# Threshold attention and MLP mixer on one core: values moved up in the unit loop, token chunk padded to 128 rows

## The chip, the cores and the metric

The kernel runs on one core of a Trainium2 chip. The metric is the device time of one execution in microseconds (us). TensorE is called PE below (PEld is its weight load), VectorE DVE, ScalarE ACT, GpSimd POOL; SP is the engine that issues most DMAs. A name with a q (SPq, ACTq) is the sequencer of that engine.

## What is computed

All data is float32; B = 8 batches, H = 8 heads, S = 576 tokens, D = 64 per head, so 512 features per token.

```python
scores = q @ k.T / 8                              # per batch and head, 576 x 576
thresh = max(scores, -1) - tau                    # tau = 0.02
scores = where(scores >= thresh, scores, -1e9)
attn = exp(scores - max(scores)); attn /= sum(attn) + 1e-9
x = (attn @ v)   ->  (B, S, 512), heads side by side
u = x + (relu(x.T @ w_tok1) @ w_tok2).T           # token MLP, 576 -> 256 -> 576
out = u + relu(u @ w_ch1) @ w_ch2                 # channel MLP, 512 -> 1536 -> 512
```

The weights are random, and each is read once from memory and kept on the chip. Where a weight arrives as 64-bit floats it is converted on the chip by ACT, DVE and POOL (`f64_to_f32`, L145).

## The kernel before, in words

**Units.** The attention is cut into 144 units (L85): for each batch b ("row" in this document), for each half of its four head pairs, nine units t = 0 to 8. A unit is one block of 128 query tokens of one head pair; t = 4 is shared: it holds the last 64 tokens of two pairs. A row therefore has 18 units. One iteration of the main loop (L513) emits, in this order, the following pieces of several units. Each engine runs what is emitted for it in order, so the order of emission is the order on each engine:

1. `scores(u)` (L272): matmuls of q by k for both heads, 64 rows high (the head size), into two PSUM tiles `sc`, and on DVE the row maximum (L291), on POOL the bias from it (L292). The pool of `sc` holds two tiles, so the next unit's scores wait until both tiles of this unit have been read (L301).
2. `norm(u - 1)` (L307): reciprocal of the row sums on DVE, the multiplication on POOL (L314).
3. For w = u - 2, from row 1 on, `turn_blocks(w)` (L341): a DVE transpose in blocks (T, L348); when a group of units is complete (units t = 1, 3, 4, 6, 8), 16 small DMAs on SP's queue (L358) that complete the transpose into a tile `eT`. Row 0 does this on PE instead (`turn`, L325). A finished group is put on the list `due`, with the iteration from which its values may be emitted: u + 2 from row 1 on, u + 1 in row 0 (L540).
4. `fill(0.4)` (L487): filler steps, see below.
5. `weight(...)`: steps of the weight conversion (L216), until all weights are there.
6. `weigh(u)` (L295): on ACT the threshold (Prelu, L301, the reader of `sc`) and the exponential (L304).
7. `fill(0.3)`.
8. The groups that are due: `values(b, p, c)` (L370): 20 PE instructions of v by `eT`, 128 rows by 64 columns, for two heads beside each other (L388, L393; a shared group has two such calls with shorter operands, tile `pv_s`), and on ACT the copy of the result (L398). After the last group of a row `push(b)` (L497) is called.
9. `fill(0.3)`, `weight(...)`, and loads of later q, k and v.

**Filler.** The mixer of a finished row is a list of steps with costs in us as the planner assumes them: `turn_x` (L405, five transposes), `tok1` (L415, two), `tok2` (L425, eight), then `channel_mlp` in chunks of 256 tokens (L440: twelve `ch1`, and four parts of `ch2` for each 128 tokens). Two chunks follow an even row, three (the last one half as long) an odd row. `push` mixes the new token steps with what is left, sets a quota of total cost / 17 for each iteration, less 45 us in all that are kept back except after row 0, and `fill(share)` pays out share times quota. After the loop everything left is emitted (L569).

**The token MLP's first matmul.** `turn_x` makes a tile `x` with 576 tokens on partitions, as four chunks of 128 and a last one of 64 (`MT`, L59). `tok1` runs one matmul for each chunk, the last one with 64 rows:

```python
for t in range(NT):
    M = MT[t]
    nc.tensor.matmul(ps, lhsT=w1[0:M, t, P * m : P * m + P], rhs=s["x"][0:M, t, :], start=(t == 0), stop=(t == NT - 1))
```

One float32 matmul is two PE instructions in the trace.

Of the kernel before, what the change touches and what calls it, by code (L numbers as in the profile page):

```python
# [9 lines left out]
F32 = mybir.dt.float32  # L10
# [7 lines left out]
P = 128  # L18
# [3 lines left out]
def kernel(  # L22
# [26 lines left out]
    nc = tc.nc  # L49
    B, H, S, D = q.shape  # L50
    DM = H * D
# [73 lines left out]
    w2 = const.tile([P, NTK, S], F32, name="w2")  # L125
    wc1 = const.tile([P, NJ, NCC, P], F32, name="wc1")
    wc2 = const.tile([P, NJ, DM], F32, name="wc2")

# [132 lines left out]
    def prep(n):  # L263
        lq, lk = loaded.pop(n)
        made = []
        for src, name in ((lq, "qT"), (lk, "kT")):
            sb = work.tile([P, S], F32, tag=name, name=f"{name}_{n}")
            nc.vector.transpose(out=sb, in_=src.rearrange("p n d -> p (n d)"))
            made.append(sb)
        heads[n] = made  # L270

    def scores(u):  # L272
        b, p0, t = units[u]
        sc = [
            (ps_3rd if b == 0 and (2 * u + h) % 3 == 2 else ps_sc).tile([P, 2, MAIN], F32, tag="sc", name=f"sc{h}_{u}") for h in range(2)
        ]
        if t == SHARED:
            parts = [(b * NP + p0 + i, slice(MAIN, S), slice(64 * i, 64 * i + 64)) for i in range(2)]
        else:
            i, c = divmod(t - (t > SHARED), NI)  # L280
            parts = [(b * NP + p0 + i, slice(P * c, P * c + P), slice(0, P))]
        order = [(f, part, h) for f in range(2) for part in parts for h in range(2)]
        for f, (n, cols, rows), h in order if b else sorted(order, key=lambda o: o[2]):
            r = slice(D * h, D * h + D)
            qT, kT = heads[n]
            nc.tensor.matmul(sc[h][rows, f, 0:HS], lhsT=qT[r, cols], rhs=kT[r, HS * f : HS * f + HS], start=True, stop=True)  # L286
        mx = small.tile([P, 2], F32, tag="mx", name=f"mx_{u}")
        bias = small.tile([P, 2], F32, tag="bias", name=f"bias_{u}")
        for h in range(2):
            c = slice(h, h + 1)  # L290
            nc.vector.tensor_reduce(out=mx[:, c], in_=sc[h][:, :, 0:HS], axis=AX.XY, op=ALU.max)  # L291
            nc.gpsimd.tensor_scalar(out=bias[:, c], in0=mx[:, c], scalar1=toff, scalar2=-SCALE, op0=ALU.add, op1=ALU.mult)  # L292
        st[u] = sc, bias
# [76 lines left out]
    def values(b, p, c):  # L370

        lv, vl = vals[b * NP + p]
        if b not in xTs:
            xTs[b] = xTs[b + 1] = work.tile([P, NP, 2 * S], F32, tag="xT", name=f"xT_{b}")
        key = (b, p - p % 2, c) if c == "s" else (b, p, c)
        n, N, tok = (1, LAST, MAIN) if c == "s" else (2, 2 * P, 2 * P * c)
        first = LAST * (p % 2) if c == "s" else 0
        eT = eTs[key] if c == "s" else eTs.pop(key)
        if in_blocks(b):
            eT = eT[:, 0 : NK * n * P].rearrange("p (i c x) -> p c i x", i=4, c=NK)  # L380
            eT = eT[:, :, first // 32 : first // 32 + N // (32 * n), :]
        else:
            eT = eT[:, 0 : NK * n * P].rearrange("p (c x) -> p c x", c=NK)[:, :, first : first + N]
        ps = ps_tr.tile([P, MAIN], F32, tag="tr", name=f"pv_{b}_{p}_{c}")[:, 0:N]
        to = ps.rearrange("p (i x) -> p i x", x=32 * n) if in_blocks(b) else ps
        for h in range(2):
            r = slice(D * h, D * h + D)
            nc.tensor.matmul(to[r], lhsT=vl[:, r], rhs=eT[:, NI], start=True, stop=False, skip_group_check=True)  # L388
        for c in range(NI):
            for h in range(2):  # L390
                r = slice(D * h, D * h + D)
                j = (NI + 1) * h + c
                nc.tensor.matmul(to[r], lhsT=lv[:, j, :], rhs=eT[:, j], start=False, stop=(c == NI - 1), skip_group_check=True)  # L393
        x = xTs[b][:, p, S * (b % 2) + tok : S * (b % 2) + tok + N]
        if in_blocks(b) and n == 2:
            x = x.rearrange("p (n i x) -> p i n x", n=n, x=32)
            ps = ps.rearrange("p (i n x) -> p i n x", n=n, x=32)
        nc.scalar.copy(out=x, in_=ps)  # L398


    def token_mlp(b):
        xT = xTs.pop(b)
        o = S * (b % 2)
        s = {}

        def turn_x(t):
            M = MT[t]
            if t == 0:
                s["x"] = work.tile([P, NT, DM], F32, tag="x", bufs=1, name=f"x_{b}")
            ps = ps_tr.tile([P, MAIN], F32, tag="tr", name=f"tx_{b}_{t}").rearrange("p (c x) -> p c x", c=NP)  # L410
            for p in range(NP):
                nc.tensor.transpose(out=ps[0:M, p, :], in_=xT[:, p, o + t * P : o + t * P + M], identity=ident)  # L412
            nc.scalar.copy(out=s["x"][0:M, t, :], in_=ps[0:M].rearrange("q p d -> q (p d)"))

        def tok1(m):  # L415
            need(2)
            if m == 0:
                s["a"] = work.tile([P, NTK, DM], F32, tag="a", bufs=1, name=f"a_{b}")
            ps = ps_mm.tile([P, DM], F32, tag="mm", name=f"t1_{b}_{m}")
            for t in range(NT):  # L420
                M = MT[t]
                nc.tensor.matmul(ps, lhsT=w1[0:M, t, P * m : P * m + P], rhs=s["x"][0:M, t, :], start=(t == 0), stop=(t == NT - 1))  # L422
            nc.scalar.activation(out=s["a"][:, m, :], in_=ps, func=AF.Relu)

        def tok2(c, f):  # L425
            need(6)
            ps = ps_mm.tile([P, HS], F32, tag="mm", name=f"t2_{b}_{c}_{f}")
            for m in range(NTK):
                nc.tensor.matmul(  # L429
                    ps, lhsT=s["a"][:, m, P * c : P * c + P], rhs=w2[:, m, HS * f : HS * f + HS], start=(m == 0), stop=(m == NTK - 1)  # L430
                )
            u = xT[:, c, o + HS * f : o + HS * f + HS]
            nc.vector.tensor_add(out=u, in0=u, in1=ps)  # L433

        steps = [(0.44, lambda t=t: turn_x(t)) for t in range(NT)]
        steps += [(4.3, lambda m=m: tok1(m)) for m in range(NTK)]
        steps += [(0.97, lambda c=c, f=f: tok2(c, f)) for c in range(NCC) for f in range(2)]
        return steps
# [58 lines left out]
    def push(b):  # L497
# [8 lines left out]
            todo.extend(channel_mlp(b - b % 2, uT, i))  # L506
        quota = (sum(c for c, _ in todo) - (KEEP if b else 0.0)) / (UB - 1)

    prep(0)
    due = deque()  # L510
    b_now = 0
    LAG = 2
    for u in range(len(units) + LAG + 4):  # L513
        on = u < len(units)
        if u == UB:
            late.close()
            ps_mm = ctx.enter_context(tc.tile_pool(name="ps_mm", bufs=2, space=bass.MemoryType.PSUM))
        if on:
            b_now, p0, t = units[u]
            n = b_now * NP + p0  # L520
        w = u - LAG
        back = 0 <= w < len(units)
        if on:
            scores(u)
        if 0 < u <= len(units):
            norm(u - 1)
        if back:
            key, place, many = group_of(w)
            if in_blocks(key[0]):
                turn_blocks(w)  # L530
            else:
                for i in range(3):
                    turn(w, i)
            if place == many - 1:
                b, p, c = key
                if c == 0 and p % 2 == 0:
                    split_middle(b * NP + p)
                if c == "s":
                    split_middle(b * NP + p + 1)
                when = u + (2 if in_blocks(b) else 1)  # L540
                due += [(when, b, p + i, c) for i in range(2 if c == "s" else 1)]
        if b_now:
            fill(0.4)
        weight(4 if b_now else 1)
        if on:
            weigh(u)
        if b_now:
            fill(0.3)
        while due and due[0][0] <= u:
            _, b, p, c = due.popleft()  # L550
            values(b, p, c)
            if p == NP - 1 and c == 1:
                push(b)
        if b_now:
            fill(0.3)
        weight(3 if b_now else 1)
        if on:
            m = n + 2 + t // 4
            if t < 8 and m < len(pairs):
                load_qk(m, (nc.scalar if b_now else nc.sync,) * 2, t % 4)  # L560
                if t % 4 == 3:
                    load_v(m)
            if t == 2:
                prep(n + 1)
            if t == 7 and n + 2 < len(pairs):
                prep(n + 2)
# [31 lines left out]
```

## Time and profile before

| what | value |
|---|---|
| median of 3 runs | 1418.58 us (1417.44 to 1421.64) |
| the profiled execution | 1424.03 us |
| its span, first to last instruction | 1421.9 us |
| mean granted PE clock | 0.984 of full speed |
| PE busy | 1346.7 us, 95% of the span |
| PEld / DVE / ACT / POOL busy | 832.4 / 584.1 / 589.8 / 345.4 us |
| largest groups on PE | L451 `ch1` 406.2 us, L467 `ch2` 389.5, L286 scores 196.7, L393 values 124.0 |
| DMA | 128.34 MB in 257376 packets, mean 90 GB/s |

The page gives the busy time of each engine as a share of the span; the span in 40 slices with tenths of busy time; the chain of work that ended last; and the groups of instructions by source line with their mean length, the idle time of their engine just before them and what ended it. A matmul's recorded length includes the time that it takes to pass through the array, during which the next one already runs, so on PE the time from one start to the next is the price of an instruction, not its length.

### The profile page before, as it was taken

The numbers are of one execution on the slowest core, as the hardware profiler recorded it, in microseconds if no ns is written. First come the engines' busy times: TensorE is split into PE (matmuls) and PEld (weight loads), VectorE is DVE, ScalarE is ACT, GpSimd is POOL, SyncE is SP. The second block draws the span as 40 slices with busy tenths as digits, with TensorE's granted clock in tenths as the row PEclk, the third lists the DMA queues.
The fourth block names the chain that finished last, engine by engine and source line by source line (L and its number), as shares of the span: only waits on it lengthen the run. The fifth ranks groups of instructions, "written<-read, shape, count | busy, mean of one in ns | idle before, by whom it ended". The sixth has DMA issues, their size and how long they took to land.

```text
span 1421.9 us, 19495 instructions
## 1 busy us (share of the span) xinstructions
PE 1346.7 (95%) x6866; PEld 832.4 (59%) x6866; DVE 584.1 (41%) x1009; ACT 589.8 (41%) x1328; POOL 345.4 (24%) x681
## 2 busy tenths in 40 slices
PE   6777689988999999999999999999999999999998
PEld 4443455645656566565656566566657466566675
DVE  5888654344344443434433444334333443201000
ACT  5776353443545444353434444353334344220110
POOL 4565332222222222222212222222121222100000
PEclk9998899989999999999999999999999999999999
DMA  6344544443444434443343534443433433300000
GB/s 130 90 117 131 152 125 103 92 116 84 102 120 111 108 84 106 104 98 80 92 101 77 121 80 111 104 98 69 103 87 83 111 91 78 82 15 15 8 8 23
DMA packets 257376, 128.34 MB, mean 90 GB/s; under 512 B 208064, under 2 KB 221376, under 8 KB 257280
## 3 DMA queue, kind: packets, MB, share of 16 engines
q1 hardware_dynamic: 131632, 111.46, 29.9%
q10 hardware_dynamic: 125648, 15.64, 6.9%
q8 instruction: 55, 0.90, 0.3%
q14 instruction: 41, 0.34, 0.1%
HBM read 43.25 MB, written 9.44 MB: 37 GB/s over the span
## 4 chain that ended last, share of the span: by engine, by line
PE 81%; DVE 8%; SPq 5%; DMA 3%; ACT 3%; issue 1%; POOL 0%; DVEq 0%; ACTq 0%
PE c L467 26%; PE c L451 24%; PE sc L286 10%; PE pv L393 7%; SPq L358 5%; PE t L422 3%; PE t L429 3%; DVE mx L291 3%; PE pv L388 2%; DVE T L348 2%; PE tx L412 2%; PE c L463 1%; DMA eT<-T 1%; DMA scratch<-in_moe_w_ch_dram 1%; ACT e L301 1%
## 5 line engine op out<-in xcount | busy, mean ns | idle before, releaser
L451 PE MATMUL c<-xT,wc 128*128 128x256 f32 (+1 forms) x1920 | 406.2, 363 | 1.9 <-DVE xT L433 0.8
L291 DVE TENSOR_REDUCE mx<-sc 128x1 f32<-128x576 f32 x288 | 204.6, 751 | 489.5 <-PE sc L286 489.4
L467 PE MATMUL c<-wc,g 128*128 128x512 f32 x864 | 389.5, 597 | 0.0
L451 PEld LDWEIGHTS c<-xT,wc 128*128 128x128 f32 x1920 | 331.7, 190 | 75.9 <-issue 29.9
L292 POOL TENSOR_SCALAR bias<-mx,toff 128x1 f32<-128x1 f32 x288 | 76.7, 267 | 807.8 <-DVE mx L291 754.1
L301 ACT ACTIVATE e<-sc,bias 128x576 f32<-128x576 f32 x288 | 199.2, 741 | 169.7 <-POOL bias L292 148.8
L467 PEld LDWEIGHTS c<-wc,g 128*128 128x128 f32 x864 | 157.6, 190 | 177.3 <-issue 175.9
L452 ACT ACTIVATE g<-c 128x256 f32<-128x256 f32 (+1 forms) x240 | 87.3, 364 | 386.0 <-PE c L451 366.5
L304 ACT ACTIVATE e<-e,ntau 128x576 f32<-128x576 f32 x288 | 220.8, 774 | 0.0
L314 POOL TENSOR_SCALAR e<-e,rr 128x576 f32<-128x576 f32 x288 | 213.4, 753 | 17.3 <-DVE rr L311 4.1
L286 PE MATMUL sc<-kT,qT 64*128 64x288 f32 (+1 forms) x1280 | 196.7, 441 | 20.0 <-ACT e L301 10.9
L348 DVE STREAM_TRANSPOSE T<-e 128x1152 f32<-128x1152 f32 x126 | 172.5, 1369 | 16.5 <-DMA eT<-T 10.8
L286 PEld LDWEIGHTS sc<-kT,qT 64*128 64x128 f32 (+1 forms) x1280 | 107.1, 181 | 102.1 <-issue 50.1
L393 PE MATMUL pv<-eT,lv 128*64 128x256 f32 x1024 | 124.0, 385 | 0.0
L472 DVE COPY o<-c 128x512 f32<-128x512 f32 x36 | 24.6, 684 | 192.7 <-PE c L467 192.7
L393 PEld LDWEIGHTS pv<-eT,lv 128*64 128x64 f32 x1024 | 75.7, 140 | 38.0 <-issue 2.6
L429 PE MATMUL t<-w,a 128*128 128x288 f32 x256 | 78.8, 437 | 17.8 <-DVE xT L433 15.8
L422 PE MATMUL t<-x,w 128*128 128x512 f32 (+1 forms) x160 | 76.0, 613 | 0.0
L429 PEld LDWEIGHTS t<-w,a 128*128 128x128 f32 x256 | 46.7, 197 | 42.6 <-DVE xT L433 20.8
L398 ACT COPY xT<-pv 128x256 f32<-128x256 f32 x64 | 23.9, 373 | 107.4 <-PE pv L393 107.3
L433 DVE TENSOR_TENSOR xT<-xT,t 128x288 f32<-128x288 f32 x64 | 27.9, 442 | 96.5 <-PE t L429 96.4
L304 ACT ACTIVATION_READ_ACCUMULATOR e<-e,ntau 128x1 f32 x288 | 57.4, 199 | 0.0
(43 smaller groups left out, 600.4 us busy)
## 6 DMA issues: line engine op xcount, KB each, us to landing
eT<-T SPq DMA_DIRECT2D x896, 72.0 KB, 2.0
scratch<-in_moe_w_ch_dram SPq DMA_DIRECT2D x24, 512.0 KB, 3.8
lv<-in_v_dram SPq DMA_DIRECT2D x32, 288.0 KB, 3.3
out_dram<-o SPq DMA_DIRECT2D x36, 256.0 KB, 2.2
eT<-T SPq DMA_DIRECT2D x224, 36.0 KB, 1.9
lk<-in_k_dram ACTq DMA_DIRECT2D x108, 72.0 KB, 2.7
lq<-in_q_dram ACTq DMA_DIRECT2D x104, 72.0 KB, 2.1
lq<-in_q_dram SPq DMA_DIRECT2D x24, 72.0 KB, 3.3
```

The lines of the kernel that those rows point to most:

```text
L286: nc.tensor.matmul(sc[h][rows, f, 0:HS], lhsT=qT[r, cols], rhs=kT[r, HS * f : HS * f + HS], start=True, stop=True)
L291: nc.vector.tensor_reduce(out=mx[:, c], in_=sc[h][:, :, 0:HS], axis=AX.XY, op=ALU.max)
L301: nc.scalar.activation(out=eh, in_=sc[h][:, :, 0:HS], func=AF.Prelu, bias=bias[:, h : h + 1], scale=SCALE, alpha=STEEP)
L304: nc.scalar.activation(out=eh, in_=eh, func=AF.Exp, bias=ntau, accum_out=rs[:, h : h + 1])
L314: nc.gpsimd.tensor_scalar(out=eh, in0=eh, scalar1=rr[:, h : h + 1], scalar2=1.0, op0=ALU.mult, op1=ALU.mult)
L348: nc.vector.transpose(out=T.rearrange("p (a c n x) -> p c a n x", a=4, c=NK, n=n)[:, :, :, place, :], in_=e.rearrange("p (c a x) -> p c a ...
L393: nc.tensor.matmul(to[r], lhsT=lv[:, j, :], rhs=eT[:, j], start=False, stop=(c == NI - 1), skip_group_check=True)
L422: nc.tensor.matmul(ps, lhsT=w1[0:M, t, P * m : P * m + P], rhs=s["x"][0:M, t, :], start=(t == 0), stop=(t == NT - 1))
L429: nc.tensor.matmul(ps, lhsT=s["a"][:, m, P * c : P * c + P], rhs=w2[:, m, HS * f : HS * f + HS], start=(m == 0), stop=(m == NTK - 1))
L451: nc.tensor.matmul(ps, lhsT=wc1[:, j, c, :], rhs=uT[:, c, GR * i : GR * i + n], start=(c == 0), stop=(c == NCC - 1))
L452: nc.scalar.activation(out=s["g"][:, j, 0:n], in_=ps, func=AF.Relu)
L467: nc.tensor.matmul(flat, lhsT=s["g"][:, j, P * t : P * t + P], rhs=wc2[:, j, :], start=False, stop=(j == NJ - 1), skip_group_check=True)
```

## The change

Two edits are made. From row 1 on, the due values are emitted directly behind `scores(u)`, ahead of `norm`, `turn_blocks`, all filler and `weigh(u)`; `push` moves with them. In row 0 they stay where they were. The due times are not changed. And the last chunk of tokens is multiplied at full height, 128 rows: `x` becomes one fixed tile `x_sb` for all rows, and the upper 64 partitions of its last chunk, and those of `w1`, are set to zero once by POOL at the start.

```diff
+    x_sb = const.tile([P, NT, DM], F32, name="x_sb")
+    nc.gpsimd.memset(x_sb[LAST:P, NI, :], 0.0)
+    nc.gpsimd.memset(w1[LAST:P, NI, :], 0.0)
...
         def turn_x(t):
             M = MT[t]
-            if t == 0:
-                s["x"] = work.tile([P, NT, DM], F32, tag="x", bufs=1, name=f"x_{b}")
...
-            nc.scalar.copy(out=s["x"][0:M, t, :], in_=ps[0:M].rearrange("q p d -> q (p d)"))
+            nc.scalar.copy(out=x_sb[0:M, t, :], in_=ps[0:M].rearrange("q p d -> q (p d)"))
...
             for t in range(NT):
-                M = MT[t]
-                nc.tensor.matmul(ps, lhsT=w1[0:M, t, P * m : P * m + P], rhs=s["x"][0:M, t, :], start=(t == 0), stop=(t == NT - 1))
+                nc.tensor.matmul(ps, lhsT=w1[:, t, P * m : P * m + P], rhs=x_sb[:, t, :], start=(t == 0), stop=(t == NT - 1))
...
+    def mix(u):
+        while due and due[0][0] <= u:
+            _, b, p, c = due.popleft()
+            values(b, p, c)
+            if p == NP - 1 and c == 1:
+                push(b)
+
...
         if on:
             scores(u)
+        if b_now:
+            mix(u)
         if 0 < u <= len(units):
             norm(u - 1)
...
-        while due and due[0][0] <= u:
-            _, b, p, c = due.popleft()
-            values(b, p, c)
-            if p == NP - 1 and c == 1:
-                push(b)
+        if not b_now:
+            mix(u)
         if b_now:
             fill(0.3)
```

## The prediction, as put on record before the run

> **What bounds the kernel now.** I read the page first: busy times, slices, chain.
>
> ```profile
> PE 1346.7 (95%) x6866; PEld 832.4 (59%) x6866; DVE 584.1 (41%) x1009; ACT 589.8 (41%) x1328; POOL 345.4 (24%) x681
> PE   6777689988999999999999999999999999999998
> PEclk9998899989999999999999999999999999999999
> PE 81%; DVE 8%; SPq 5%; DMA 3%; ACT 3%; issue 1%; POOL 0%; DVEq 0%; ACTq 0%
> ```
>
> PE is full from about 200 us on; before that it waits for others. Next, the busy time by stage (columns: length, then busy time of PE, PEld, DVE, ACT, POOL with counts, PE clock, DMA share, GB/s):
>
> ```profile
> 100.00:205.00 105.00, 77.71 (x373) 49.06 (x372) 76.29 (x118) 57.63 (x119) 46.49 (x61) 0.85 0.50 138
> 300.00:310.00 10.00, 3.84 (x18) 2.29 (x20) 6.46 (x12) 5.85 (x12) 4.40 (x10) 0.69 0.62 158
> 480.00:810.00 330.00, 328.26 (x1694) 200.77 (x1693) 134.14 (x227) 137.31 (x314) 76.69 (x164) 1.00 0.40 95
> ```
>
> Up to 205 us (row 0 and the weight conversion) PE idles. At 300 to 310 us there is one hole, the end of row 1. Elsewhere a microsecond added to PE or taken from it is a microsecond of the span. So two things count: what PE's stream costs, and whether PE, which runs in order, meets a wait.
>
> The PE timeline of one iteration shows the stream:
>
> ```profile
> 600.15 1.24 PE L286 MATMUL sc<-kT,qT 64*128 64x288 f32 x8
> 601.32 3.72 PE L451 MATMUL c<-xT,wc 128*128 128x256 f32 x16
> 604.97 0.65 PE L388 MATMUL pv<-eT,vl 128*64 128x256 f32 x4
> 605.45 1.90 PE L393 MATMUL pv<-eT,lv 128*64 128x256 f32 x16
> 607.28 1.99 PE L451 MATMUL c<-xT,wc 128*128 128x256 f32 x8
> 609.20 1.20 PE L286 MATMUL sc<-kT,qT 64*64 64x288 f32 x16
> ```
>
> The numbers behind the line are the shape of the array in use: 64*128 for scores, 128*128 for filler, 128*64 for values. The starts of single instructions give the price of a change of shape. Inside a run of L451, starts lie 216 ns apart; from its last one to another shape 309 ns (+93); and the first one of a run is followed after 320 ns (+104). A change into full shape or into scores costs 93 + 104 = 197 ns, one into values 93 + 51 = 144 ns (261 for 210). From scores straight to values it is 333 ns for 242, the same 91.
>
> The other side is the DMA chain that values wait for, in the SP timeline and in the answer on L358:
>
> ```profile
> 605.21 11.10 SPq L358 DMA_DIRECT2D eT<-T  x16
> L358 SPq DMA_DIRECT2D eT<-T x1120: 507/589/1937, 136.8 to 1242.6; - x187
> DMA to landing us min/median/max: 1.8/2.0/5.5
> ```
>
> Sixteen issues take about 10 us; the last lands 2 us later. Over all 70 groups, first issue to last landing is 12.05 us on average (11.3 to 13.1). The first issue stands 4.31 us after the start of the scores of its iteration, nearly always. So values of iteration u can't start before s(u-2) + 16.4 us, with s the start of scores.
>
> **What the Trainium skill says.** "TensorEngine Tiling (Array Packing)", Key Properties: changing the tiling mode drains TensorE. The trace agrees: 93 ns at each change. "TensorE: Matmul & The Clock Gate", "What overlaps and what doesn't": weight loads overlap running matmuls only in other row groups; that page also has loads pulled ahead into a background buffer. The trace shows the overlap lost just behind a change of shape (+104). The same page, "Why this matters for your kernels": PE gaps above some 3 us bring the clock to half. Here the hole of 301 to 308 us did it (clock 0.69 in the table), gaps of 1.7 us at 338 and 346 us didn't.
>
> **The change, part by part.**
>
> *Shape changes.* Before, an iteration with values runs scores, filler, values, filler; after, scores, values, filler. One re-entry into filler goes: 197 ns. I followed the planner's costs and credit on paper through both orders: of the 70 iterations with values from unit 18 on, 47 have filler behind the values and save it; in 23 the order changes without fewer changes of shape. 47 x 0.197 = 9.3 us.
>
> *Full height.* The two forms of L422:
>
> ```profile
> L422 PE MATMUL t<-x,w 128*128 128x512 f32 x128 | 59.2, 606 | 0.0
> L422 PE MATMUL t<-x,w 64*128 64x512 f32 x32 | 18.0, 641 | 0.0
> ```
>
> By starts, full height costs 429 ns; the step into the 64-row pair 522, between its two instructions 533, out of it 519. Per `tok1` that is 93 + 104 in excess, and 90 + 51 or 104 more where no scores follow (scores have 64 rows too, no change). Afterwards a tok1 in front of scores pays 197 there. Summed over 16 calls: 4.5 before, 2.6 after, 1.9 us saved. In several places the last 64-row matmul overlapped with scores of the other half (a 14 ns start distance); that is lost, at most 0.43 x 4, say 1 us. Both together: 9.3 + 1.9 - 1 = **-10 us**. The two memsets: 128x128 takes 202 ns on POOL (L121); these are 64x512 and 64x256, at most 0.4 us each, while POOL waits for the first scores at 9 us: nothing, and 0.8 us without that cover.
>
> *Landing.* Values come at s(u) + 1.2 instead of behind 70% of the filler. The landing doesn't move, so iterations u-2 and u-1 must last 15.2 us together. Group by group in the trace of before, I compared landing and end of scores. The cover after the change is 2 to 5 us in rows 4 and 6, 0 to 3 in rows 3, 5 and 7, and missing in row 2, whose iterations are short (6.5 to 8 us without values). There the landing is late by 1.3, 2.2, 2.4, 4.2, 2.2 and 0.7 us (iterations 46, 48, 52, 53, 55, 57). A wait at one is a head start for a group already under way: 1.3 + 0.9 + 2.4 + 1.9 + 0.3 + 0.4 = 7.1 us. Walking the new filler slots with the prices above gives 8.4 in row 2, 5.9 in rows 3 to 7 (single waits of 0.3 to 1.8), and 4.6 at iterations 145 and 147, where no scores stand between: 18.9. About 1 us of this exists before (0.7 at 436 us). **+18 us**; with 11.5 us to landing +12, with 12.6 us +27. Moved instructions on SP: none, since turn_blocks and its DMAs stay behind scores. The wait stands in PE's queue, with the filler queued behind it, and on ACT behind the copy of the values.
>
> *ACT.* The copy L398 (373 ns) and its wait now come ahead of `weigh(u)`: Prelu starts about 1.5 us later, 2.3 where filler on ACT comes between. Exp still ends before the next norm needs it. The next scores need both Prelus done; before, 2.2 us of values hid them where all filler fell into the first slot. That cover is gone, 2 us each. But push comes 0.7 of an iteration earlier, so the long tok1 steps fall elsewhere; the walk finds one new wait (iteration 61, 1.8) and two of 0.4 gone: **+1 us**. Bounds: 0 to +8.
>
> *Row 0 and 1.* Push of row 0 is 0.7 of an iteration earlier, and PE has room there. By iteration 27 two more ch2 steps (5.2 us) are done, if the weights set the pace. Against it, filler runs out an iteration earlier at the end of row 1:
>
> ```profile
> 308.06 1.12 PE L388 MATMUL pv<-eT,vl 128*64 128x256 f32 x4 [4.93 <-DMA eT<-T]
> ```
>
> This wait of 4.9 us, with 2.0 ahead of it, grows to some 10. Net **-3 us** (between -4 and +2, if ACT's order holds up the weights).
>
> *Clock.* One or two more gaps of 3 us at half clock: **+1 us** (0 to +5).
>
> Sum: -10 + 18 + 1 - 3 + 1 = **+7 us**: the profiled 1424.0 becomes 1431. The median of the runs is 5.4 us below the profiled one; there, 1418.6 + 7 = **1425.6 us**.
>
> **Rivals.** *Shape changes win* (the other side): the place is rows 2, 3, 5 and 7; the price -10 - 3 against landing waits. The waits decide from about 13 us on; if they are 7, because landing takes 11.5 us and part of them replaces stalls that row 2 has anyway (1.7 us twice at 338 and 346 us, for the adds of tok2), it is -6: 1413 us. For it: 46 of the 68 groups that scores follow would have been in time with over 1 us to spare; the issues take 9.4 us when undisturbed. Against it: row 2 is short whatever happens. *Landing with half clock*: groups at 12.6 us (SP's issues slow to 10.5 us when q and k load), waits of 27, half clock twice: +9 more and some, 1436. For it: six groups of row 2 in the trace took 12.4 to 13.0. *They cancel*: waits of 12, 1419.
>
> **Chances.** Forecast 0.45, shape changes win 0.20, landing heavy 0.25, cancel 0.10. A measurement of this kernel can tell about 0.3%, 4.3 us, from no change. Slower by more: 0.33 of the forecast and the heavy case, 0.58. Within: 0.11 of the forecast, the cancelling 0.10, 0.04 of the first rival: 0.25. Faster: 0.16, and 0.01 of the forecast for an error in the early part: 0.17. The range takes in most of both rivals: 1411 to 1439. The forecast's own: 1421 to 1431.
>
> **What would show it.** L422 with one form at 429 ns steps. Changes of shape fewer by some 60, about 12 us of PE time. Idle before L388 "<-DMA eT<-T" of 15 to 30 us, half of it between 310 and 450 us. Idle before L286 on ACT e up by 2 us at most. Wrong if PE's wait at L388 stays under 10 us or goes over 35, or if scores wait for ACT by 10 us.

## The result and the profile after

| | before | after |
|---|---|---|
| median of 6 runs each | 1420.85 us | 1432.19 us (1429.75 to 1434.82) |
| ratio, 95% interval | | 1.008 (1.0057 to 1.0103) |
| span of the profiled execution | 1421.9 us | 1431.8 us |

The change makes the kernel slower by 11.3 us in the medians and by 9.9 us in the two profiles. First the page of the changed kernel: PE's busy time, its slices and granted clock, and the chain.

```profile
PE 1343.2 (94%) x6866; PEld 843.0 (59%) x6866; DVE 585.0 (41%) x1009; ACT 586.0 (41%) x1328; POOL 347.9 (24%) x683
PE   6777889978999999999999999999999999999998
PEclk9996999989999999999999999999999999999999
PE 75%; SPq 8%; DVE 7%; DMA 4%; ACT 3%; issue 2%; POOL 1%; ACTq 0%; DVEq 0%; POOLq 0%
```

PE does the same work in slightly less busy time (1343.2 for 1346.7 us), yet the span is longer: PE waits more. The chain says for what: SP's queue went from 5% to 8%, PE fell from 81% to 75%. The windows (length, then busy time of PE, PEld, DVE, ACT and POOL with counts, PE clock, DMA share, GB/s), the first two in the weight phase and at the end of row 1:

```profile
100.00:205.00 105.00, 82.90 (x387) 53.12 (x385) 75.70 (x119) 55.94 (x116) 45.76 (x60) 0.82 0.49 137
302.00:312.00 10.00, 5.51 (x21) 3.50 (x23) 5.30 (x8) 2.84 (x6) 3.51 (x8) 0.50 0.56 138
480.00:810.00 330.00, 324.03 (x1683) 201.43 (x1682) 131.18 (x221) 137.89 (x319) 75.46 (x160) 1.00 0.40 95
```

From 480 to 810 us, where the clock is full, PE is busy 4.2 us less than in that window before. A stretch of row 2 in the PE timeline shows the new order and the new waits (in brackets: idle time before the instruction, and what ended it):

```profile
415.10 1.24 PE L290 MATMUL sc<-kT,qT 64*128 64x288 f32 x8
418.60 0.65 PE L392 MATMUL pv<-eT,vl 128*64 128x256 f32 x4 [2.26 <-DMA eT<-T]
419.05 1.93 PE L397 MATMUL pv<-eT,lv 128*64 128x256 f32 x16
420.91 5.45 PE L452 MATMUL c<-xT,wc 128*128 128x256 f32 x24
426.29 1.24 PE L290 MATMUL sc<-kT,qT 64*128 64x288 f32 x8
...
439.64 1.31 PE L290 MATMUL sc<-kT,qT 64*128 64x288 f32 x8
443.33 0.65 PE L392 MATMUL pv<-eT,vl 128*64 128x256 f32 x4 [2.38 <-DMA eT<-T]
```

Values now follow scores, filler runs in one piece, and at 418 us PE stands still in front of the values although 24 filler instructions are queued behind them. The SP timeline of that stretch (two groups of issues without a break), the answer on landing, and PE's waits (us in all, times, longest), first after and then before:

```profile
406.63 20.15 SPq L362 DMA_DIRECT2D eT<-T  x32
```

```profile
L362 SPq DMA_DIRECT2D eT<-T x1120: 507/589/1786, 142.9 to 1255.2; - x187
DMA to landing us min/median/max: 1.8/2.0/5.7
```

```profile
PE sc L290 <- ACT e L305: 22.7, 10, 5.2
PE pv L392 <- DMA eT<-T: 15.4, 9, 3.7
```

```profile
PE sc L286 <- ACT e L301: 10.9, 6, 3.4
PE pv L388 <- DMA eT<-T: 5.5, 2, 4.9
```

The DMA chain itself is as it was (median issue 589 ns, landing after 2.0 us; the first issue 4.31 us behind the scores in 47 of the 70 groups, before in 45). PE's wait for it rose from 5.5 us in two places (4.9 of them the hole at 308 us) to 15.4 in nine. Scores wait for ACT 11.8 us longer too. Of that, 1.3 us lie between 310 and 1260 us (1.3 before, 2.6 after); the rest lies in rows 0 and 1. From 115 to 200 us this wait rose from 7.1 to 12.4 us, but PE's waits there fell from 23.4 to 17.7 us in all, because the token MLP's instructions wait less (15.8 before, 5.3 after).

To add up the whole span I took the starts of all PE instructions and split the time from the first of them on into four parts: **work** (each instruction at its start distance at full clock without a change of shape), **changes of shape** (counted, at the prediction's price of 93 ns, and 104 or 51 ns behind it), **idle** (PE's recorded gaps), and the **rest**, mostly half clock: the half-clock windows in the clock records last 44.4 us before and 61.4 after. Work is 1223.8 us in every kernel here. Where stretches of iterations are compared below, an iteration starts with its scores; iteration 39 starts with its values instead, so the hole at the end of row 1 belongs to iterations 20 to 38.

| us | changes of shape (number) | idle | rest |
|---|---|---|---|
| before | 80.6 (437) | 62.3 | 42.4 |
| after | 68.6 (376) | 75.5 | 50.9 |
| difference | -12.0 (-61) | +13.2 | +8.5 |

The sum is +9.7 of the 9.9 us. The idle before values behind 305 us alone, whatever it is put down to, went from 5.5 to 18.9 us.

### The profile page after: what moved, and what is told of

It is laid out like the page before. It is cut to its first block, busy times and chain, and to the rows that moved or that the text cites. A ratio compares the mean times of both kernels' runs of the same rounds, so it can differ in the third digit from the quotient of the medians.

```text
span 1431.8 us, 19564 instructions
## 1 busy us (share of the span) xinstructions
PE 1343.2 (94%) x6866; PEld 843.0 (59%) x6866; DVE 585.0 (41%) x1009; ACT 586.0 (41%) x1328; POOL 347.9 (24%) x683
## 4 chain that ended last, share of the span: by engine, by line
PE 75%; SPq 8%; DVE 7%; DMA 4%; ACT 3%; issue 2%; POOL 1%; ACTq 0%; DVEq 0%; POOLq 0%
PE c L452 23%; PE c L468 22%; PE sc L290 9%; SPq L362 8%; PE pv L397 7%; PE t L423 5%; PE t L430 3%; DVE mx L295 3%; PE pv L392 2%; DMA eT<-T 2%; DVE T L352 1%; ACT e L305 1%; PE tx L414 1%; DMA lk<-in_k_dram 1%; PE c L464 1%
## 5 line engine op out<-in xcount | busy, mean ns | idle before, releaser
L452 PE MATMUL c<-xT,wc 128*128 128x256 f32 (+1 forms) x1920 | 401.9, 362 | 5.0 <-ACT g L453 2.8
L290 PE MATMUL sc<-kT,qT 64*128 64x288 f32 (+1 forms) x1280 | 198.3, 445 | 31.9 <-ACT e L305 22.7
L397 PE MATMUL pv<-eT,lv 128*64 128x256 f32 x1024 | 130.4, 399 | 0.0
L397 PEld LDWEIGHTS pv<-eT,lv 128*64 128x64 f32 x1024 | 80.9, 144 | 38.2 <-issue 5.8
L430 PE MATMUL t<-w,a 128*128 128x288 f32 x256 | 75.6, 424 | 8.0 <-DVE xT L434 6.7
L423 PE MATMUL t<-x_sb,w 128*128 128x512 f32 x160 | 73.7, 608 | 0.0
L392 PE MATMUL pv<-eT,vl 128*64 128x256 f32 x256 | 43.6, 419 | 20.0 <-DMA eT<-T 15.4
```

The lines of the kernel that those rows point to most:

```text
L423: nc.tensor.matmul(ps, lhsT=w1[:, t, P * m : P * m + P], rhs=x_sb[:, t, :], start=(t == 0), stop=(t == NT - 1))
L430: nc.tensor.matmul(ps, lhsT=s["a"][:, m, P * c : P * c + P], rhs=w2[:, m, HS * f : HS * f + HS], start=(m == 0), stop=(m == NTK - 1))
L452: nc.tensor.matmul(ps, lhsT=wc1[:, j, c, :], rhs=uT[:, c, GR * i : GR * i + n], start=(c == 0), stop=(c == NCC - 1))
```

## The experiments

Theory: PE, running in order, now meets the values before their 16 DMAs have landed. Rivals: full height costs something; the order on ACT or the earlier `push` does. Each diff is against the changed kernel. Each measured median stands beside that of the kernel before on the same chip; the ratio of the two has its 95% interval behind it.

**Full height alone.** In the loop, values go back behind the filler.

```diff
-        if b_now:
-            mix(u)
...
-        if not b_now:
-            mix(u)
+        mix(u)
```

> Full height alone; values stay behind the filler. My theory (the values' new place makes PE wait for the transposing DMAs, and costs about 9 to 12 us; full height is harmless): about 15 changes of shape fewer than before, 2.9 us, idle of PE as before; against the kernel before -1 to -4 us, so 1417 to 1420 us where before has 1420.8. Rival (full height itself costs, through the fixed tile or the memsets at the start): 1425 us or more, with the excess before 205 us or at the L423 group.

Measured: 1418.5 us for 1421.54, ratio 0.9976 (0.9967 to 0.9986), so some 3 us less. Changes of shape are 77.6 us (422), 3.0 less than before; idle is 62.7, as before. Full height is not the loss; alone it gains what its changes of shape are worth.

**The move alone.** Tile `x` and `M = MT[t]` are as before; the values move up.

> The values' new place alone; the last chunk keeps 64 rows. My theory: nearly the whole effect, +10 to +15 us against before (1431 to 1436), PE idle before the values 15 to 25 us, about 10.6 us less in changes of shape (54 fewer). Rival (full height costs): not over +5 us.

Measured: 1436.27 us for 1421.54, ratio 1.0103 (1.0081 to 1.0124). Changes of shape are 69.9 us (383), idle is 76.6. The loss belongs to the move.

**One more iteration for the DMAs.**

```diff
-                when = u + (2 if in_blocks(b) else 1)
+                when = u + (3 if in_blocks(b) else 1)
```

> Both parts, but from row 1 on a group is due one iteration later, so that its DMAs have some 8 us more. If the wait for landing is the cause, idle before the values falls from 20 us to under 4 (the end of row 1 apart, where the hole may grow by 3 us because filler runs out earlier), the savings in changes of shape stay, and the time falls to 1408 to 1418 us, at or below before. If the cause is the order on ACT (weigh behind the values' copy, scores waiting for the scores' tiles), or the earlier push, it stays at 1428 to 1434 us.

Measured: 1411.58 us for 1421.54, ratio 0.9919 (0.9902 to 0.9937): 10 us faster than before, with the same 376 changes of shape as the changed kernel. Idle before values behind 305 us is 0.6 us. The order on ACT is that of the changed kernel; `push` comes an iteration later, so this run alone does not rule out the earlier `push`. The scores' wait for ACT is even longer than in the changed kernel (22.7 us), so it isn't what makes that one slow:

```profile
PE sc L290 <- ACT e L305: 25.6, 12, 6.9
```

**Row 2 at the old place.**

```diff
-        if b_now:
+        if b_now and b_now != 2:
             mix(u)
...
-        if not b_now:
+        if not b_now or b_now == 2:
             mix(u)
```

> Both parts, but in the 18 iterations of row 2 (where quota is smallest) the values stand at their old place. The theory that row 2's short iterations make the loss: waits of 6 us there go, 2 us of changes of shape come back, a wait of 2.4 us at the first values of row 3 may stay: 5 to 8 us faster than the changed kernel, 1424 to 1427 us. If landing waits of all rows or the early part count as much, less than 3 us.

Measured: 1420.42 us for 1421.54, ratio 0.9989 (0.998 to 0.9997), 12 us below the changed kernel's median, more than the 5 to 8 expected. In iterations 39 to 56 idle falls from 11.7 to 6.4 us and the rest from 6.9 to 3.0, changes of shape rise by 0.6. A further 3.7 us come from iteration 143 on (idle 2.6 to 0.4, the rest 1.5 less), where the filler steps fall otherwise and the wait at 1246 us goes. Row 2 is the main place, and its price includes the clock.

**Values in front of the next scores.** The other side of scores is also a neighbour: `mix` moves to the end of the iteration.

```diff
             scores(u)
-        if b_now:
-            mix(u)
...
         weight(3 if b_now else 1)
+        if b_now:
+            mix(u)
```

> Both parts, due times as in the change, but from row 1 on the values are emitted last in their iteration, so just ahead of the next unit's scores instead of just behind their own. The values still stand beside scores, so as many changes of shape go (about 60, 12 us), and their DMAs have more time than at the old place. If the changed kernel's loss is landing alone: waits at the values under 3 us outside the end of row 1, total 1406 to 1413 us. If the savings come only together with a later due time or an earlier push, or scores then wait for ACT: 1416 us or more.

Measured: 1405.2 us for 1420.78, ratio 0.9887 (0.9869 to 0.9906): 15.6 us below before. Changes of shape are 68.6 us (376), idle is 57.3. The hole at the end of row 1 now stands at 300 us, with 1.7 us of idle before its values; behind it no values wait at all. The PE timeline of the same stretch as above:

```profile
418.52 3.72 PE L452 MATMUL c<-xT,wc 128*128 128x256 f32 x16
422.18 0.65 PE L392 MATMUL pv<-eT,vl 128*64 128x256 f32 x4
422.66 1.90 PE L397 MATMUL pv<-eT,lv 128*64 128x256 f32 x16
424.48 1.24 PE L290 MATMUL sc<-kT,qT 64*128 64x288 f32 x8
425.65 5.45 PE L452 MATMUL c<-xT,wc 128*128 128x256 f32 x24
```

The order is filler, values, scores, filler: one block of filler for each iteration, as in the change, with the filler as cover for the DMAs. It gained more than the changes of shape: iterations 20 to 38 took 183.1 us for 192.6 before, with the same work. Why the weight phase profits was not separated.

**Half as many DMAs.**

```diff
-                for i in range(4):
+                for i in range(2):
                     nc.sync.dma_start(
-                        out=eTs[key][32 * a : 32 * a + 32, w * i : w * i + w], in_=T[32 * i : 32 * i + 32, w * a : w * a + w]
+                        out=eTs[key][32 * a : 32 * a + 32, 2 * w * i : 2 * w * i + 2 * w],
+                        in_=T[64 * i : 64 * i + 32, w * min(a, 2) : w * min(a, 2) + 2 * w],
```

> The changed kernel with 8 DMAs of double width in place of 16 for each group, the same bytes and the same order of everything else (it moves wrong blocks, so attention from row 1 on is computed from misplaced values). Issue should take about 5 us instead of 10 and landing come at some 11.5 us instead of 16.4 us after the scores. If PE's waits are the length of SP's issues: idle before values under 3 us outside the end of row 1, total 1408 to 1416 us. If the order on ACT or the push is the cause: 1428 us or more.

Measured: 1405.29 us for 1420.78, ratio 0.9884 (0.9863 to 0.9906), 3 us below the range expected. The order of all else is the changed kernel's, with 376 changes of shape. The SP timeline and the landing:

```profile
400.53 4.94 SPq L362 DMA_DIRECT2D eT<-T  x8
```

```profile
L362 SPq DMA_DIRECT2D eT<-T x560: 507/589/2057, 142.7 to 1224.4; - x187
DMA to landing us min/median/max: 1.9/2.7/5.2
```

An issue costs what it cost before, 589 ns at twice the width, so a group takes 4.9 instead of 10 us, and 7.6 instead of 11.9 us from its first issue to its last landing. Behind the hole at the end of row 1, which now stands at 300 us with 2.9 us of idle, no values wait any more. This takes away the cause and leaves the order on ACT and the place of `push`: the wait was the length of SP's issues. The gain of 26.9 us against the changed kernel is more than that wait. In the two profiles 19.0 us of it come from iteration 39 on, and 8.9 lie in iterations 20 to 38, where the weight loads share SP's queue. ACT's waits for those loads, in the changed kernel and then with half the DMAs:

```profile
ACT scratch L163 <- DMA scratch<-in_moe_w_ch_dram: 11.4, 2, 6.5
```

```profile
ACT scratch L163 <- DMA scratch<-in_moe_w_ch_dram: 1.8, 3, 0.9
```

Weight loads stand in the queue behind 16 issues, which may be what ACT waited for. But with the values in front of the next scores, and 16 issues a group, this wait was small as well (4.0 us), so the number of issues is not shown to be all of it:

```profile
ACT scratch L163 <- DMA scratch<-in_moe_w_ch_dram: 4.0, 3, 2.8
```

**Old place, later due time.** Full height alone, with groups due at u + 3.

> Full height, values at their old place, due one iteration later. A control for the run with the later due time: if its gain comes from fewer changes of shape, this one has some 379 of them and stays at the time of full height alone, 1416 to 1421 us. If the later due time itself gives the gain (less waiting anywhere), it comes to 1408 to 1413 us.

Measured: 1424.32 us for 1420.78, ratio 1.0021 (1.0012 to 1.0031), 3 us above the range expected. Changes of shape stay at 422. The later due time gives nothing by itself; against full height alone it costs some 6 us in the medians and 4.3 in the profiles. The hole at the end of row 1 is not the place: counted from the scores of iteration 39, idle in iterations 39 to 56 is 11.3 us here and 11.5 with full height alone. 2.2 us of added idle lie in iterations 57 to 142, mostly matmuls of the mixer that wait for DVE's additions; the remainder was not traced to a cause. The control holds: the gain of the run with the later due time came with fewer changes of shape, not from the due time.

**The move from row 2 on, and the change again on the same chip.**

```diff
-        if b_now:
+        if b_now > 1:
             mix(u)
...
-        if not b_now:
+        if b_now < 2:
             mix(u)
```

> The change as it is, but the values move up from row 2 on only; in row 1 they stay behind the filler. This prices the early part, which the prediction put at -3 us. If that holds, this kernel is 3 us slower than the changed one. The traces since then (192.6 us for iterations 20 to 38 before, 191.8 after) say within 1 us, and if the earlier push or the order on ACT costs time in the weight phase, it is 2 us or more faster.

> The changed kernel unaltered, on the same chip as the run beside it, for the comparison: 1430 to 1434 us, and again 376 changes of shape and 13 us more idle PE than before.

Measured: 1434.97 and 1434.15 us, ratios 1.0098 (1.0076 to 1.0119) and 1.0092 (1.0073 to 1.011), where before had 1421.06. Moving the values in row 1 too is worth 0.8 us, not 3, and with four runs each, which overlap (1433.4 to 1435.9 and 1432.8 to 1435.3), that is not clear of zero. The changed kernel repeats its 376 changes and its 14 us of added idle.

## Why the prediction came out as it did

The time, 1432.2 us, lies in the range and on the side forecast. The mechanism forecast, PE waiting for landing at the new place, is what the runs show. The sum of +7 us was too small by 4 in the medians and by 3 in the profiles, and the median lies just above the forecast's own 1421 to 1431; 2.3 us of that come from the kernel before, whose median of six runs is 1420.85 and not 1418.6. By its steps, with the two profiles:

- **Changes of shape**, -10: measured -12.0, and 61 fewer where the followed order said some 60. The price of 197 ns stands in the starts after, too. The count of 47 holds: full height alone has 422 changes, full height and the move 376, so 46 fewer. Full height was put at 1.9 us; alone its 15 changes make 3.0. The microsecond set aside for lost overlap does not show in its median, which is also 3.0 us lower. The two memsets took 0.5 and 0.3 us and were done at 2.7 us, ahead of PE's first scores at 9.2.
- **Landing**, +18: the idle before values, without the hole at the end of row 1 (4.9 before, 3.7 after), went from 0.6 to 15.2 us, so by 14.6. Nearly all of the places are those named: 8.5 us in row 2 (8.4 from the walk), 4.1 in rows 3 to 7 (5.9), 2.6 at the end (4.6). In row 2 PE waited in iterations 48, 52, 53 and 55 as listed, and in 44 in place of 46; 57 had no wait. Twelve microseconds to landing was the right figure: 11.9 on average (11.3 to 14.2). The shorter DMA chain and the later due time both removed the wait. (The six head starts add up to 7.2, not 7.1; the sum did not use them.)
- **ACT**, +1: the wait of scores for ACT behind 310 us rose by 1.3 us. Over the whole span it rose by 11.8, where the prediction allowed 2 and called 10 a sign of being wrong. That sign appeared and was not the loss: the added wait stands in rows 0 and 1, where PE's waits in all fell from 61.0 to 58.4 us (up to 310 us). It goes when row 1 is left at the old place (12.8 us), without a gain in time, and with the later due time it is longer in a kernel that is 10 us faster than before.
- **Row 0 and 1**, -3: this step failed in size. The two extra ch2 steps were done by iteration 27 (work in iterations 20 to 26 went from 53.7 to 59.3 us), but those iterations took 93.0 us for 90.4: PE had less free room there than assumed. Iterations 20 to 38 together gained 0.8 us: idle fell by 4.3 and changes of shape by 1.9, and the rest, mostly half clock, took back 5.4. Iterations 0 to 19 took 2.0 us longer (106.4 to 108.4), where the forecast had nothing. 1.2 of it lie in iterations 0 to 17, which the move does not touch; there the run with row 2 at the old place, whose code is the same up to that point, took what before took (89.3 and 89.2 us, after 90.4), so this is chance. 0.8 lie in iterations 18 and 19, where values of row 0 already stand at the new place and the scores behind them wait 3.9 us for ACT, 0.5 before.
- **Clock**, +1 with a bound of 5: mis-sized. The rest of PE's time rose by 8.5 us: 5.4 in iterations 20 to 38, which the step before already holds, 2.8 from 39 on. Two new windows of 3.4 us at half clock start at 387 and 1247 us, just behind waits of 2.0 and 2.6 us.

By stage the forecast was 0, -3 and +10 for iterations 0 to 19, 20 to 38 and from 39 on; measured are +2.0, -0.8 and +8.5. That the sum comes so near is partly luck: landing was put 3 us too high and the gain from changes of shape 2 too low, and both hid a part of what the early stages and the clock cost.

The first rival, that changes of shape win, had the right price for what is saved: with the landing wait gone the same order is 10 to 16 us faster than before. It lost because the wait stayed above its 13 us. The heavy rival's mechanism (12.6 us to landing) did not occur, but its clock part did. The Trainium skill's "TensorEngine Tiling (Array Packing)", Key Properties, was cited for the drain at each change of shape, 93 ns in these traces; fewer of them are what full height alone gained (3 us), and a part of what the move to the end of the iteration gained.

## What to carry to other kernels

On an engine that runs in order and is full, ask of every instruction that is moved up whether its inputs are there at the new place; the cover it leaves behind is worth as much as the place. When two blocks should stand beside each other to save changes of array shape, try both sides: behind the scores cost 11 us here, in front of the next scores gained 16, with equally many changes of shape (376). Count a chain of small DMAs by the issues on its queue, and look for what else waits in that queue.

## What was not expected of the hardware

- In the changed kernel the clock went to half behind waits shorter than the 3 us that the prediction cites: 2.0 us (row 2) and 2.6 us (at 1247 us), while waits of 2.3 and 2.4 us at 418 and 443 us had no such window. Length alone doesn't decide.
- What separates them in these traces is the place of the wait. The half-clock windows of all runs start and end at points of one grid of 3.41 us. The changed kernel, its repeat, the move alone and the move from row 2 on have 16 waits of 2.0 us or more behind 310 us. Eight of them (2.0 to 2.7 us) leave a stretch of the grid in which PE is busy for 1.4 us or less, and half clock follows each. The other eight (2.3 to 2.6 us) are all cut in two by the grid and leave 1.6 us or more in each stretch, and none follows. This is no full rule: before, the window at 324 us follows a stretch with 2.1 us of busy time.
- A DMA of twice the width costs SP the same 589 ns to issue; the median landing rose from 2.0 to 2.7 us.
